# Decay sums without padding, gathered by two DMAs, in an RWKV-6 attention and maxout kernel

## The chip, the cores and the metric

The kernel runs on one core of a Trainium2 chip. A core has TensorE (PE, with its weight loads shown apart as PEld), VectorE (DVE), ScalarE (ACT), GpSimd (POOL) and SyncE (SP), each with its own instruction queue, and 16 DMA engines that move data between the core's memories and HBM. The metric is device time in microseconds (us) of one execution.

## The reference

The first part is a linear attention with a decay for each channel, the second a feed-forward layer without a bias:

```python
# r, k, v, w: (B=4, H=8, S=768, D=48); u: (H, D)
for t in range(S):
    cur = einsum('bhd,bhe->bhde', u[None] * kt, vt)
    y[:, :, t] = einsum('bhd,bhde->bhe', rt, state + cur)
    state = wt[:, :, :, None] * state + einsum('bhd,bhe->bhde', kt, vt)
x = y.transpose(0, 2, 1, 3).reshape(B * S, H * D)        # 3072 x 384
out = maximum(x @ w1, x @ w2) @ w_out                    # d_ff = 1024
```

## The kernel before

The time axis is cut into three segments of 256 steps (`SEG`). Two neighbouring steps sit in one partition, so that a segment fills 128 partitions. A unit is one segment of one or two batches (`UNITS`): units 0 to 3 are the first segment of one batch each, units 4 and 5 the second segment of two batches each, units 6 and 7 the last segment. In each unit the recurrence is turned into matrix products: scores of r against k under a mask, products with v, and a state per head (`S_f`, 48 x 48 values) that passes from one segment to the next.

The decay runs through the logarithm. `wp` multiplies the decays of the two steps of a pair, `ln` takes the logarithm into `lg`, `ex` sums `lg` over the earlier partitions on PE with the triangle `tri`, `e0` exponentiates this sum in place (`E`), and `mz` (line 323, DVE) adds `lg` to the sum, which gives the sum up to and with the partition's own pair: `MZ`. This has one buffer for all units. `ie` (line 329, ACT) makes exp(-MZ), the factor by which k is scaled.

The last partition of `MZ` holds the sum over the whole segment, one value for each channel. The state needs its exponential as a column: channel on the partition. Six units (all but the two of the last segment) therefore do the following. `row` (line 334, SP) copies partition 127 of `MZ` to DRAM, as one row. `wl` (line 338, SP) reads it back with one element per partition and column: this is the gather. `we` (line 342, ACT) takes the exponential into `W`, and `sm` (line 451, POOL or DVE) multiplies the state by it. The next segment's `st` (line 445) adds to this state.

A head has 48 channels and is kept on 64 partitions (`DP`), two heads to the 128 partitions (`NP` = 4 pairs): head 2p on partitions 0 to 47, head 2p+1 on 64 to 111, and 16 partitions of zeros behind each. Before the change `MZ` itself has 64 columns for each head, of which the last 16 are set to zero once (`zero.m`, lines 185 and 198, DVE), and the row in DRAM is H x 64 = 512 values for each batch. One DMA then spreads them: 128 partitions by 4 columns for a unit of one batch, by 8 for two.

The order of all work is written out by hand in `ORDER`: each entry names an operation, its unit and, behind the @, the engine (a ACT, d DVE, p POOL). An engine does its part of the list in that order. Every plain DMA goes through SP, except two of the last stores: the loads of w, k, r, v (line 297, one for each batch), the weights (237 and 242), the row and the gather, the transposes of `dt` (line 412, from unit 5 on) and the stores of the result (568, 570). The gathers of units 0 and 1 stand among the loads of units 2 and 3, those of 2 and 3 among the loads of units 4 and 5; unit 4's is followed by `row.5`, `os.0.0`, `load.7.w` and `dt.5.0.1`, and ACT does `we.4` just ahead of `xe.4.0`, whose tile `xT` the matmuls `gt.4` (line 530, PE) read. The feed-forward layer is `gt` (line 530), `rl` (540 or 542), `op` (549 and 553) and `oe` (148). The launch code behind line 597 allocates the tensors and is not touched.

Of the kernel before, what the change touches and what calls it, by code (L numbers as in the profile page):

```python
# [8 lines left out]
F32 = mybir.dt.float32  # L9
BF16 = mybir.dt.bfloat16  # L10
AF = mybir.ActivationFunctionType
# [4 lines left out]
@with_exitstack  # L16
def kernel(
    ctx: ExitStack,
    tc: tile.TileContext,
    r: bass.AP,  # L20
    k: bass.AP,
    v: bass.AP,
    w: bass.AP,
    u: bass.AP,
    moe_w1: bass.AP,
    moe_w2: bass.AP,
    moe_w_out: bass.AP,
    out: bass.AP,
):
    nc = tc.nc  # L30
    with tc.manual_schedule(), nc.allow_non_contiguous_dma(reason="one row moved onto partitions"):
        _body(tc, r, k, v, w, u, moe_w1, moe_w2, moe_w_out, out)
# [63 lines left out]
def _body(tc, r, k, v, w, u, moe_w1, moe_w2, moe_w_out, out):  # L96
    nc = tc.nc
    B, H, S, D = r.shape
    P = 128
    Q = P // 2  # L100
    HD = H * D
# [3 lines left out]
    NP = H // 2  # L105
    DP = 64
# [7 lines left out]
    const = tc.alloc_tile_pool(name="cst", bufs=1)  # L114
    wk = tc.alloc_tile_pool(name="wk", bufs=1)
    drp = tc.alloc_tile_pool(name="dr", bufs=2, space=bass.MemoryType.DRAM)
    ps = tc.alloc_tile_pool(name="ps", bufs=1, space=bass.MemoryType.PSUM)

    def wt_(shape, dt, tag, bufs=1):
        return wk.tile(shape, dt, tag=tag, name=tag, bufs=bufs)  # L120
# [14 lines left out]
    vp_ = [const.tile([P, 2, NP, 2, VP], BF16, name=f"vp{i}") for i in range(3)]  # L135
    identq = const.tile([P, Q], BF16)
    M_ = [[const.tile([P, 2, NP, 2, Q], BF16, name=f"M{j}{i}") for i in range(3)] for j in range(2)]
    MZ = const.tile([P, 2, H, DP], F32)
    S_f = const.tile([P, 2, B, NP, D], F32)
    S_b = const.tile([P, 2, B, NP, 2, D], BF16)  # L140
    wd_sb = const.tile([P, KO, d_ff], BF16)
# [34 lines left out]
    def c_zero(*a):  # L176
        x, e = a[0], a[-1]
        n = a[1] if len(a) == 3 else 0

        def zero(t):  # L180
            if e == "a":
                k = t.shape[1]
                nc.scalar.copy(t, zw[:, 0:t.shape[2]].unsqueeze(1).to_broadcast([P, k, t.shape[2]]))
            else:
                (nc.vector if e == "d" else nc.gpsimd).memset(t, 0.0)

        if x == "r":
            zero(rp_[n][:, :, :, :, D:].rearrange("p b i h d -> p (b i h) d"))
        elif x == "k":
            zero(kp_[n][:, :, :, :, D:].rearrange("p b i h d -> p (b i h) d"))  # L190
        elif x == "v":
            t = vp_[n].rearrange("p b q e x -> p (b q e) x")
            zero(t[:, :, D:DP])
            zero(t[:, :, DP + D:])
        elif x == "M":
            zero(M_[n % 2][n // 2].rearrange("p e a i g -> p (e a) (i g)"))
        elif x == "m":
            zero(MZ.rearrange("p b h d -> p (b h) d")[:, :, D:])
        else:
            zero(S_b[:, n].rearrange("p b q e d -> p (b q) (e d)"))  # L200

# [117 lines left out]
        nc.scalar.activation(t, t, AF.Exp)  # L319

    def mz(s, b):
        s.mz = MZ[:, 0:s.nb]
        nc.vector.tensor_add(MZ[:, b, :, 0:D],
                             getattr(s, f"E{b}").rearrange("p (h d) -> p h d", h=H),
                             s.lg[:, b].rearrange("p (h d) -> p h d", h=H))

    def ie(s):
        s.iE = wt_([P, 2, HD], F32, "iE", 2)[:, 0:s.nb]
        nc.scalar.activation(s.iE.rearrange("p b (h d) -> p (b h) d", h=H),  # L329
                             s.mz.rearrange("p b h d -> p (b h) d")[:, :, 0:D], AF.Exp, scale=-1.0)  # L330

    def row(s):
        s.row = drp.tile([1, 2 * H * DP], F32, tag="row", name="row")[:, 0:s.nb * H * DP]
        nc.sync.dma_start(out=s.row, in_=MZ[P - 1:P, 0:s.nb].rearrange("o b h d -> o (b h d)"))

    def wl(s):
        s.WL = wt_([P, 2 * NP], F32, "WL", 2)[:, 0:s.nb * NP]
        nc.sync.dma_start(out=s.WL, in_=s.row.rearrange("o (a x) -> x (o a)", x=P))  # L338

    def we(s):  # L340
        s.W = wt_([P, 2 * NP, 1], F32, "W", 2)[:, 0:s.nb * NP]
# [220 lines left out]
    def os(s, a):  # L562
# [6 lines left out]
        else:  # L569
            (nc.scalar if i else nc.sync).dma_start(out=dst[:, i, :], in_=t[:, i])  # L570

    ops = {"tri": c_tri, "ident": c_ident, "mask": c_mask, "zero": c_zero, "u": u_load,
           "uspread": u_spread, "utake": u_take, "ones": c_ones, "warm": warm,
           "wload": w_load, "woload": wo_load, "wdiff": w_diff, "w2cast": w2_cast,
           "wocast": wo_cast, "w2turn": w2_turn, "w2take": w2_take, "wfold": w_fold,
           "wctake": wc_take}
    unit = {"wp": wp, "ln": ln, "ex": ex, "e0": e0, "mz": mz, "ie": ie, "row": row, "wl": wl,
            "we": we, "rk": rk, "ru": ru, "dg": dg, "di": di, "rw": rw, "kw": kw, "vb": vb,
            "scale": scale, "tr": tr, "te": te, "kv": kv, "st": st, "sm": sm, "sb": sb, "sc": sc,
            "mk": mk, "yi": yi, "ya": ya, "xe": xe, "gt": gt, "rl": rl, "op": op,  # L580
            "oe": oe, "os": os, "load": load, "dt": dt}
    for o in ORDER:
        o, _, e = o.partition("@")
        name, *a = o.split(".")
        a = [int(x) if x.isdigit() else x for x in a] + ([e] if e else [])
# [39 lines left out]
```

## Time and profile before

| | |
|---|---|
| median of 3 runs | 146.85 us |
| the three runs | 147.11, 143.3, 146.85 us |
| the profiled execution, its own time | 146.0 us |
| its span, first to last instruction | 144.3 us |
| mean granted TensorE clock | 1.000 |
| PE, DVE, ACT, POOL busy | 133.0, 110.7, 99.3, 77.1 us |
| DMA | 70790 packets, 31.84 MB, mean 221 GB/s |
| gathers, line 338 | six, landing 4.2 to 7.7 us after issue |

How to read the profile: the busy share of an engine is the time in which it has an instruction under way. The slices cut the span into 40 equal parts, with a digit for the tenths busy in each. Groups show the count, the total busy time and the mean duration of one. A wait names the instruction whose end, by the semaphores, released the waiting one. The chain of work that ended last is followed back from the last instruction, at each step to what released it. SPq is the queue of SP: its instructions issue DMAs, and their length is the time until SP goes on to the next, not the transfer's, which has its own time from issue to landing.

### The profile page before, as it was taken

The page shows a single profiled execution, that of the slowest core. Times are in us where ns is not written, and L with a number is a line of the kernel's source. Part 1 is how long each engine was busy: PE and PEld are TensorE (multiplying, and loading weights), DVE is VectorE, ACT ScalarE, POOL GpSimd, SP SyncE. Part 2 cuts the span into 40 slices and gives each one's busy share as a digit, 9 for nine tenths or more (in the row PEclk, how much of TensorE's full clock was granted, in tenths as well). Part 3 has the DMA queues.
Part 4 walks back from the last instruction along what each step waited for, and adds up shares of the span by engine and source line. Part 5 has one row for each costly group of instructions (what it writes and reads, how often), then busy time and mean ns, then how long its engine had stood idle before and what let it go on. Part 6 is the DMA issues. An engine that isn't in the chain of part 4 may idle for free.

```text
span 144.3 us, 5437 instructions
## 1 busy us (share of the span) xinstructions
PE 133.0 (92%) x2378; PEld 80.6 (56%) x2378; DVE 110.7 (77%) x133; ACT 99.3 (69%) x168; POOL 77.1 (53%) x73
## 2 busy tenths in 40 slices
PE   6995569999999999999999989979999999999991
PEld 2333354577777857765754557435567546654560
DVE  0499989989999989989997999966996599040110
ACT  7869799999799899749946937666582752238211
POOL 8828529880691198459494698909786520000000
PEclk9999999999999999999999999999999999999999
DMA  4999999999999997979999999997909960005032
GB/s 104 312 338 311 351 305 347 320 323 244 321 306 268 268 227 180 263 196 277 244 270 211 177 336 344 209 183 169 337 12 160 215 250 7 0 7 218 8 118 95
DMA packets 70790, 31.84 MB, mean 221 GB/s; under 512 B 67175, under 2 KB 68712, under 8 KB 70766
## 3 DMA queue, kind: packets, MB, share of 16 engines
q1 hardware_dynamic: 70478, 31.10, 83.6%
q8 instruction: 18, 0.29, 0.8%
q10 hardware_dynamic: 288, 0.39, 0.7%
q14 instruction: 6, 0.05, 0.1%
HBM read 23.61 MB, written 4.73 MB: 196 GB/s over the span
## 4 chain that ended last, share of the span: by engine, by line
PE 41%; DVE 20%; DMA 19%; issue 6%; SPq 5%; ACT 4%; POOL 2%; DVEq 0%
PE G L553 13%; PE G L530 11%; DMA lw<-in_w_dram 6%; DVE M L474 6%; PE G L549 5%; DVE rku L152 5%; DMA lk<-in_k_dram 5%; DMA lv<-in_v_dram 4%; DMA lr<-in_r_dram 4%; SPq L338 4%; PE G L224 3%; PE Y L512 3%; PE E L315 2%; PE Y L467 2%; DVE dg L355 2%
## 5 line engine op out<-in xcount | busy, mean ns | idle before, releaser
L553 PE MATMUL G<-wo_sb,gT 128*128 128x384 bf16 x192 | 35.1, 326 | 0.0
L530 PE MATMUL G<-xT,wd_sb 128*128 128x256 bf16 (+1 forms) x192 | 33.8, 326 | 0.3 <-DVE wd_sb L248 0.2
L540 ACT ACTIVATE gT<-G 128x512 bf16<-128x512 f32 x44 | 25.5, 597 | 11.4 <-PE G L530 10.6
L474 DVE CAST_PREDICATED M<-mask,Y 128x1024 bf16<-128x1024 int32 x24 | 28.5, 1216 | 2.4 <-PE Y L467 2.3
L553 PEld LDWEIGHTS <-gT 128*128 128x128 bf16 x192 | 18.8, 98 | 12.4
L530 PEld LDWEIGHTS <-wd_sb 128*128 128x128 bf16 x192 | 18.2, 98 | 12.8 <-DVE wd_sb L248 0.8
L152 POOL TENSOR_TENSOR kp<-lk,iE 128x768 bf16<-128x768 f32 x11 | 20.1, 1845 | 6.0 <-ACT iE L329 5.6
L148 ACT COPY osb<-G 128x384 f32<-128x384 f32 x21 | 9.8, 479 | 12.9 <-PE G L553 12.4
L152 POOL TENSOR_TENSOR lg<-lw 128x768 f32<-128x768 f32 (+1 forms) x6 | 9.5, 1579 | 12.3 <-DMA lw<-in_w_dram 11.3
L152 POOL TENSOR_TENSOR M<-identq,dg 128x512 bf16<-128x512 bf16 x13 | 14.3, 1110 | 3.2 <-DVE dg L355 3.2
L549 PE MATMUL G<-wc_sb,xT 128*128 128x384 bf16 x72 | 15.8, 328 | 0.0
L152 DVE TENSOR_TENSOR rku<-lr,lk 128x768 f32<-128x768 f32 x12 | 13.3, 1125 | 1.5 <-DMA lk<-in_k_dram 0.7
L224 PE MATMUL G<-zw 128*128 128x512 bf16 x40 | 11.6, 428 | 1.4 <-DVE zw L219 1.2
L315 PE MATMUL E<-lg,tri 128*128 128x384 f32 x24 | 10.4, 509 | 2.3 <-issue 1.2
L148 ACT CAST vp<-lv 128x768 bf16<-128x768 f32 x12 | 9.9, 827 | 2.6 <-DMA lv<-in_v_dram 2.4
L152 POOL TENSOR_TENSOR lr<-lr,lw 128x768 f32<-128x768 f32 (+1 forms) x5 | 7.4, 1488 | 7.8 <-DVE rku L152 7.8
L152 DVE TENSOR_TENSOR rp<-lr,E 128x768 bf16<-128x768 f32 x12 | 11.3, 943 | 0.0
L148 ACT COPY qk<-G 128x1024 bf16<-128x1024 bf16 x11 | 11.0, 1008 | 0.4 <-PE G L399 0.4
L355 DVE TENSOR_REDUCE dg<-rku 128x16 f32<-128x768 f32 (+1 forms) x8 | 10.7, 1343 | 0.1
L152 POOL TENSOR_TENSOR rku<-rku,u_b 128x768 f32<-128x768 f32 x5 | 9.1, 1823 | 2.9 <-DVE rku L152 2.9
L467 PE MATMUL Y<-qk 48*64 48x128 bf16 x384 | 8.6, 220 | 1.1 <-DVE M L474 0.7
L148 ACT CAST xT<-Y 128x768 bf16<-128x768 f32 x9 | 7.2, 797 | 3.5 <-PE Y L512 2.8
(79 smaller groups left out, 191.2 us busy)
## 6 DMA issues: line engine op xcount, KB each, us to landing
lw<-in_w_dram SPq DMA_DIRECT2D x12, 384.0 KB, 6.0
lr<-in_r_dram SPq DMA_DIRECT2D x12, 384.0 KB, 5.5
lk<-in_k_dram SPq DMA_DIRECT2D x12, 384.0 KB, 5.0
lv<-in_v_dram SPq DMA_DIRECT2D x12, 384.0 KB, 5.8
out_dram<-osb SPq DMA_DIRECT2D x10, 384.0 KB, 3.5
gT<-in_moe_w_dram SPq DMA_DIRECT2D x4, 512.0 KB, 6.5
lv<-in_moe_w_out_dram SPq DMA_DIRECT2D x4, 384.0 KB, 5.1
wst<-in_moe_w_dram SPq DMA_DIRECT2D x2, 512.0 KB, 6.1
```

Of the source, the lines that this page charges most:

```text
L148: (nc.scalar.copy if e == "a" else nc.vector.tensor_copy if e == "d" else nc.gpsimd.tensor_copy)(o, i)
L152: (nc.vector if e == "d" else nc.gpsimd).tensor_mul(o, a, b)
L224: nc.tensor.matmul(t.rearrange("p (a t) -> p a t", t=P), zw, zw.unsqueeze(1).to_broadcast([P, 4, P]), start=True, stop=True, skip_group_ch ...
L315: nc.tensor.matmul(t[:, 0:HD], tri, s.lg[:, b])
L338: nc.sync.dma_start(out=s.WL, in_=s.row.rearrange("o (a x) -> x (o a)", x=P))
L355: nc.vector.reduce_sum(s.dg.rearrange("p b h o -> p (b h) o"), s.rku.rearrange("p b h i d -> p (b h i) d"), axis=AX.X)
L467: nc.tensor.matmul(t[q * Q:(q + 1) * Q, e, p * P:(p + 1) * P].rearrange("s (i g) -> s i g", i=2), turned(s, 1, b)[d, j, p, q, :], turned(s ...
L474: nc.vector.copy_predicated(t.rearrange("s e p t -> s (e p) t"), mask[:, j].rearrange("s i g -> s (i g)").bitcast(mybir.dt.int32).unsqueez ...
L530: nc.tensor.matmul(t[:, m * n * P:(m + 1) * n * P].rearrange("c (b t) -> c b t", t=2 * P), wd_sb[:, ko, fo * P:(fo + 1) * P], s.xT[:, 0:s. ...
L540: nc.scalar.activation(o, i, AF.Relu)
L549: nc.tensor.matmul(t[:, 0:HD], s.xT[:, b, ko, i * P:(i + 1) * P], wc_sb[:, ko, :], start=(ko == 0), stop=False)
L553: nc.tensor.matmul(t[:, 0:HD], s.gT[:, c:c + P], wo_sb[:, f, :], start=False, stop=(f == FO - 1))
```

## The change

`MZ` loses its padding: 48 columns for each head. The sum of `mz` and the exponential of `ie` then run over tiles without gaps. The row in DRAM has 384 values for each batch. The gather becomes two DMAs, one for the even heads to partitions 0 to 47 and one for the odd heads to 64 to 111. Since the 16 partitions behind each are no longer written by the gather, the target is a tile `WL_` of its own with two slots, which the units take in turn, and `zero.m` sets this tile to zero instead of the padding of `MZ`. `ORDER` stays as it is.

```diff
-    MZ = const.tile([P, 2, H, DP], F32)
+    MZ = const.tile([P, 2, H, D], F32)
+    WL_ = const.tile([P, 2, 2 * NP], F32)
...
         elif x == "m":
-            zero(MZ.rearrange("p b h d -> p (b h) d")[:, :, D:])
+            zero(WL_)
...
     def mz(s, b):
-        s.mz = MZ[:, 0:s.nb]
-        nc.vector.tensor_add(MZ[:, b, :, 0:D],
-                             getattr(s, f"E{b}").rearrange("p (h d) -> p h d", h=H),
-                             s.lg[:, b].rearrange("p (h d) -> p h d", h=H))
+        s.mz = MZ[:, 0:s.nb].rearrange("p b h d -> p b (h d)")
+        nc.vector.tensor_add(s.mz[:, b], getattr(s, f"E{b}"), s.lg[:, b])
 
     def ie(s):
         s.iE = wt_([P, 2, HD], F32, "iE", 2)[:, 0:s.nb]
-        nc.scalar.activation(s.iE.rearrange("p b (h d) -> p (b h) d", h=H),
-                             s.mz.rearrange("p b h d -> p (b h) d")[:, :, 0:D], AF.Exp, scale=-1.0)
+        nc.scalar.activation(s.iE, s.mz, AF.Exp, scale=-1.0)
 
     def row(s):
-        s.row = drp.tile([1, 2 * H * DP], F32, tag="row", name="row")[:, 0:s.nb * H * DP]
+        s.row = drp.tile([1, 2 * HD], F32, tag="row", name="row")[:, 0:s.nb * HD]
         nc.sync.dma_start(out=s.row, in_=MZ[P - 1:P, 0:s.nb].rearrange("o b h d -> o (b h d)"))
 
     def wl(s):
-        s.WL = wt_([P, 2 * NP], F32, "WL", 2)[:, 0:s.nb * NP]
-        nc.sync.dma_start(out=s.WL, in_=s.row.rearrange("o (a x) -> x (o a)", x=P))
+        s.WL = WL_[:, s.n % 2, 0:s.nb * NP]
+        src = s.row.rearrange("o (a e d) -> e d (o a)", e=2, d=D)
+        for e in range(2):
+            nc.sync.dma_start(out=s.WL[e * DP:e * DP + D], in_=src[e])
```

## The prediction

> **What bounds the kernel now.** I read the page's busy shares and slices first, then the stretches of time, then the chain of work that ended last, and last the queue of SP around line 338, the only engine work that the change adds to.
>
> Busy shares and slices:
>
> ```profile
> PE 133.0 (92%) x2378; PEld 80.6 (56%) x2378; DVE 110.7 (77%) x133; ACT 99.3 (69%) x168; POOL 77.1 (53%) x73
> PE   6995569999999999999999989979999999999991
> DMA  4999999999999997979999999997909960005032
> ```
>
> PE is at nine tenths or more from 22 us almost to the end, but for two slices (at 83 and 94 us), and the DMA engines are full up to about 70 us. So there are two stages: loads and PE together up to about 85 us, and PE alone after that.
>
> The stretches of time (PE, PEld, DVE, ACT and POOL busy, then clock, DMA share and GB/s):
>
> ```profile
> 10.00:15.00 5.00, 2.92 (x32) 1.56 (x33) 4.97 (x6) 4.62 (x7) 3.72 (x4) 1.00 1.09 314
> 35.00:40.00 5.00, 5.00 (x69) 3.84 (x68) 4.88 (x8) 4.09 (x9) 2.65 (x2) 1.00 1.15 313
> 70.00:75.00 5.00, 4.89 (x35) 2.76 (x28) 4.96 (x5) 3.29 (x7) 3.66 (x3) 1.00 1.01 241
> 90.00:95.00 5.00, 3.76 (x80) 2.10 (x63) 3.93 (x4) 3.25 (x6) 3.86 (x2) 1.00 1.18 208
> ```
>
> PE has real holes at 10 to 20 us (about 4 us) and at 90 to 95 us (1.24 us). From 25 us to 140 us all its holes sum to 2.7 us. This caps what any relief after 25 us can bring.
>
> The chain, the pieces that touch the changed code:
>
> ```profile
> 7.96 0.27 DVE MZ L185
> 14.71 0.48 DVE MZ L323
> 28.35 4.45 SPq L338
> 53.59 0.64 SPq L338
> 72.41 5.71 DMA lw<-in_w_dram
> ```
>
> Line 338 is the gather that is now split in two. It sits on the chain twice, 5.09 us together, as SP's queue. One of the two pieces is 4.45 us long.
>
> The gather's own view, and where its result is waited for:
>
> ```profile
> L338 SPq DMA_DIRECT2D WL<-row x6: 693/1220/4452, 20.8 to 99.2; - x6
> DMA to landing us min/median/max: 4.2/4.6/7.7
> 71.17 0.79 ACT L148 CAST xT<-Y 128x768 bf16<-128x768 f32 x1
> 73.57 0.21 ACT L342 ACTIVATE W<-WL 128x8 f32<-128x8 f32 x1 [1.62 <-DMA WL<-row]
> 73.69 0.78 ACT L148 CAST xT<-Y 128x768 bf16<-128x768 f32 x1
> 73.60 0.81 PE L315 MATMUL E<-lg,tri 128*128 128x384 f32 x2
> 74.52 1.67 PE L530 MATMUL G<-xT,wd_sb 128*128 128x512 bf16 x7
> ```
>
> Of six gathers, one is waited for: that of unit 4, issued at 68.91 us, landed at 73.55. ACT stands 1.62 us, does the exponential, then casts xT (ends 74.47), and PE starts gt.4.4 on it at 74.52, after the matmul before it ended at 74.41. So at this one place a later landing moves PE, with 0.1 us to spare.
>
> **The change part by part.** The profiled execution took 146.0 us with a span of 144.3; the median of the three runs is 146.85, so the sum below is made on a run 0.6% under the median, and the runs differ among themselves by 2.6% (143.3 to 147.11). A measurement of this kernel tells about 2% from no change, that is, under 143.9 or over 149.8.
>
> *Memset.* 128x256 becomes 128x16 elements: from 272 ns to about the 112 ns of the smallest DVE memset on the page (zw, 128x64), so 0.16 us less on DVE at 8 us. It is a chain piece, and row.1 waits on SP for mz.1 (2.0 us, to 15.21). But the loads behind it go to DMA engines that are full (share 1.09 at 10 to 15 us), so what is late next is the load of lr. Bounds 0 and -0.16; I take 0.
>
> *mz and ie without gaps.* The padded sum takes 551 ns; the same shape without padding, S_f<-Y,S_f at line 445, takes 553. The exponential of 128x768 takes 835 ns, the logarithm of an unpadded 128x768 840. Zero for both.
>
> *The row to DRAM.* 2 or 4 KB become 1.5 or 3 KB. The packet records have one packet per row, 84 ns for one of 2 KB. Under 0.05 us in a landing of some us; zero.
>
> *Fewer gathered elements.* 512 become 384 for the four one-batch units, 1024 become 768 for the two others: 4096 packets of 4 bytes become 3072. The packet records show 9 ns each, over 16 engines 0.58 us less of DMA time in all. In the stages where DMA is full lie five of the six gathers; at most -0.5, at least 0. I take 0, since PE has the holes only before 20 us, where no gather is yet.
>
> *One more issue per unit, six in all.* The floor is the shortest issues of SP: 0.25 us for a row, 0.37 for a load. The ceiling is the gather itself, median 1.22, and 4.45 for the worst. The long issues are not work of SP: the same load takes 0.37 in one place and 2.14 in another, just where the engines are full, so an issue lasts until there is room for its packets. Two halves with a quarter fewer packets need less room, and what is left is the fixed part; nearest are the load and the row: I take 0.4 each. For wl.0 to wl.3 it is covered by transfers already under way (loads land a median 5.6 us after issue) and by their results' slack: W is computed at 28.46, 38.03, 55.08 and 58.56 without a wait for the gather. Without that cover the four would cost 1.6. For wl.5 the landing at 103.43 has 7.5 us to its use at 110.94, and behind it on SP the transposes wait 4.7 us for POOL anyway: 0. For wl.4 there is no cover: the second half lands 0.4 later, ACT's W, then xT, then gt.4.4 shift: +0.4 less the 0.1 to spare, with nothing given back: I keep 0.4. Bounds here -0.5 (a shorter burst) and +1.2. Queued behind it on SP are row.5, the store os.0.0 and the two loads of lw at 71.99; POOL waits 2.1 us for these already and has a hole of 1.5 us behind, so 0.4 is covered there.
>
> *The rotation of SP's semaphores.* In the trace each DMA of SP waits for the landing of the eighth before it. Six more DMAs make this the seventh in old numbering, for eight issues after each gather. Counted so, the smallest margin among the recorded landings is 0.78 us (lr at 27.32). No wait; up to +0.5 if the timing shifts, taken as 0.
>
> *Clearing the two slots.* WL is now written in two slots of one tile; each slot was last read two units before, as with the two buffers. Zero; its failure is rival C.
>
> Sum: 146.0 + 0.4 = 146.4.
>
> A rule speaks against this change. The Trainium skill, page "DMA: Bandwidth & Descriptors", section "Rules for kernel authors", says that two transfers to disjoint partition halves serialize, and to use one transfer over 128 partitions; its anatomy of one DMA gives about 2.0 us of fixed cost (a fit for another issue path). As an estimate from that page the sum would be 146.0 + 2.0 = 148.0. The trace of before has no split gather, so it does not settle this; rival B prices it from rows.
>
> **The rivals.**
>
> B, the halves follow one another in full. The second then lands a full issue (1.08, the gather at 68.91) and a burst later (0.9 to 1.5 us in the packet records) than the one gather did: +2.0 to +2.6 at wl.4, 148.3. For it: landings of 4.6 us for 4 KB show a queue in order. Against: the first half has fewer packets. This is the page's case above.
>
> C, the second half waits for the first to land (both write one tile). At wl.4 that is a whole landing, +4.6 less 0.1, 150.5; if the two chain places at 28 and 53 us pay 4.2 each too, 158.9. Against: the two loads of a two-batch unit write one tile and leave SP back to back (lw at 71.99 and 72.41).
>
> D, slower: SP is itself the bound, and the second issue costs what the first does. Place: the two chain pieces of line 338. Doubled they add 5.09: 151.1; with the median issue, 1.22, at these two and wl.4, 149.7. It decides from 1 us per issue at these three places. For it: SP has hardly a hole up to 100 us, and 4.45 us lie on the chain. Against: the issue lengths follow the DMA load, and PE is 4.6 to 5.0 of 5.0 busy there.
>
> E, faster: with less room needed, the 4.45 us shrinks to the shortest gather issue, 0.69: -3.76, 142.2. Against: PE's holes after 25 us are 2.7 us in all. If the block only shrinks by the quarter of packets, 5.09 x 0.25 = 1.3 less, 144.7, which is case F.
>
> **How the numbers follow.** Forecast 0.47 (its own range 145.0 to 147.6), B 0.14, C 0.07, D 0.18, E 0.06, F 0.08. Faster: E, and 0.04 of F and of the forecast's spread, since one of three runs before was already at 143.3: 0.10. Slower: C, D less the 0.02 that stay under 149.8, and 0.03 of B's upper end: 0.26. Within 2%: the remaining 0.64. The predicted time is the forecast's, 146.4. The range goes from 143.4 (F with 1.3 more from the spread of runs) to 151.2 (D in full); it leaves out E, the upper part of C and some ends, under 0.2.
>
> **What would show it.** Right: twelve issues at the gather's lines, the second of each pair near 0.4 us where DMA is not full, the pair's sum at 28 us no longer than 4.5 to 5; W of unit 4 on ACT waiting 1.6 to 2.4 us, gt.4.4 0.3 to 0.5 later against the matmuls before it; PE's busy time unchanged at 133. Wrong: a wait of SP of 4 us between the halves (C), pairs whose sum is twice the old issue (D), a landing 2 us later (B), a hole of PE that closes before 85 us (E). The whole is wrong if transfers elsewhere shift by more than their slack, above all the loads at 22 to 28 us, where a margin of 0.8 us is all there is.

## The result and the profile after

The changed kernel takes 150.77 us in the median of six runs (149.19 to 151.26), the kernel before 146.53 us of six (143.3 to 148.0). The ratio is 1.045, with an interval of 1.033 to 1.057: slower by more than 2%, and each of the six lies above each of the six before. The ratio is taken over the runs that lie within 1.5% of the fastest of their kernel, and since the kernel before spreads more widely (two of its six are within) it comes out above the ratio of the medians, 1.029; I give both below. The profiled execution of the changed kernel took 150.66 us, with a span of 149.0.

Busy shares, slices and the main DMA queue of the page of the changed kernel:

```profile
PE 135.3 (91%) x2378; PEld 82.2 (55%) x2378; DVE 109.7 (74%) x133; ACT 98.9 (66%) x168; POOL 76.8 (52%) x73
PE   6996568797999779999999999979999999999992
DMA  4999999998999999999989899999946970005022
q1 hardware_dynamic: 69550, 31.10, 87.3%
```

The same queue before the change:

```profile
q1 hardware_dynamic: 70478, 31.10, 83.6%
```

The same 31.10 MB in 928 fewer packets keep the engines busy for longer: 87.3% of 149.0 us is 130.1 us for each of the 16, where 83.6% of 144.3 was 120.6. No term of the prediction adds DMA time. PE's new holes lie between 22 and 56 us.

Where it begins is told by the stretches of time (PE, PEld, DVE, ACT, POOL busy, then clock, DMA share, GB/s). After:

```profile
5.00:10.00 5.00, 5.00 (x18) 2.17 (x17) 3.38 (x8) 3.69 (x7) 2.81 (x9) 1.00 1.20 297
10.00:15.00 5.00, 3.44 (x26) 1.78 (x24) 4.77 (x6) 3.99 (x6) 3.12 (x3) 1.00 1.24 289
50.00:55.00 5.00, 3.00 (x67) 2.38 (x66) 4.96 (x6) 2.60 (x5) 0.06 (x1) 0.92 0.95 242
55.00:60.00 5.00, 5.00 (x43) 3.03 (x42) 2.99 (x5) 3.65 (x8) 4.32 (x3) 0.74 1.08 244
```

Before, for the first of them:

```profile
5.00:10.00 5.00, 5.00 (x20) 1.98 (x19) 3.92 (x8) 3.61 (x7) 2.81 (x9) 1.00 1.08 325
```

From 5 to 15 us the engines are fuller (1.20 and 1.24 against 1.08 and 1.09) and move less (297 and 289 GB/s against 325 and 314). The first gather is issued at 21.75 us. So the loss starts before the first instruction that the change adds (the second half of that gather, at 23.89 us). A share above 1 means that packets of one engine overlap in time.

The gathers themselves, after:

```profile
L338 SPq DMA_DIRECT2D WL__89<-row x12: 435/1030/4237, 21.7 to 105.4; - x12
DMA to landing us min/median/max: 3.5/4.1/4.7
```

and SP around the first two pairs:

```profile
21.75 2.58 SPq L338 DMA_DIRECT2D WL__89<-row  x2
24.44 0.80 SPq L298 DMA_DIRECT2D lw<-in_w_dram  x1
25.28 2.55 SPq L238 DMA_DIRECT2D wst<-in_moe_w_dram  x1
30.97 4.72 SPq L338 DMA_DIRECT2D WL__89<-row  x2
35.79 0.24 SPq L332 DMA_DIRECT2D row<-MZ  x1
```

Twelve issues, the second of each pair 0.43 to 0.92 us, no wait between the halves, and a pair's sum of 4.72 us where the single one took 4.45. The gather lands no later after its issue than before.

What the late loads do is seen in the waits, ACT's and then PE's line of the time order at 52 us (the last bracket is the idle time before, and what ended it):

```profile
52.16 0.83 ACT L149 CAST vp<-lv 128x768 bf16<-128x768 f32 x1 [2.56 <-DMA lv<-in_v_dram]
53.05 0.44 PE L429 MATMUL Y<-vp,kp 64*64 64x48 bf16 x32 [2.00 <-ACT vp L149]
```

v arrives late, ACT casts it late, and PE stands for 2.00 us at a place where before it had no hole. After this the granted clock is 0.74 in the mean of five microseconds. One of the six runs of the changed kernel has a mean clock of 1.000 and takes 150.89 us, so the clock is not what the loss hangs on.

Theory P (placement) was formed from these rows. `MZ` has become 1024 bytes shorter in each partition and `WL_` takes 64, so the tiles allocated behind them start 960 bytes earlier (the last two, `W` and `xT`, behind the old place of `WL`, 1024). In the allocation of the two programs the buffers of the loads (lw, lr, lk, lv) start at multiples of 512 bytes before the change, and 64 bytes past one after it. A load is made of rows of 384 bytes, one packet each. The packet records of the traces show these 49152 packets:

| kernel | load buffers, past a multiple of 512 | mean, ns | at 22 ns | above 22 |
|---|---|---|---|---|
| before | 0 | 22.9 | 97.9% | 1.2% |
| after | 64 | 26.3 | 54.6% | 44.5% |

The packets that are neither at 22 ns nor above it take 20 or 21. 49152 x 3.4 ns over 16 engines are 10.4 us more of each engine's time, about the 9.5 us above. The rival, theory S, is the prediction's case D: the split itself, through SP.

### The profile page after: what moved, and what is told of

It reads as the page before. It is cut to its first block, busy times and chain, and to the rows that moved or that the text cites. A ratio compares the mean times of both kernels' runs of the same rounds, so it can differ in the third digit from the quotient of the medians.

```text
span 149.0 us, 5446 instructions
## 1 busy us (share of the span) xinstructions
PE 135.3 (91%) x2378; PEld 82.2 (55%) x2378; DVE 109.7 (74%) x133; ACT 98.9 (66%) x168; POOL 76.8 (52%) x73
## 3 DMA queue, kind: packets, MB, share of 16 engines
q1 hardware_dynamic: 69550, 31.10, 87.3%
## 4 chain that ended last, share of the span: by engine, by line
PE 66%; DMA 18%; SPq 6%; ACT 4%; DVE 3%; issue 1%
PE G L553 19%; PE G L530 18%; DMA gT<-in_moe_w_dram 9%; DMA lv<-in_v_dram 8%; PE G L549 8%; PE E L316 4%; PE Y L512 4%; PE Y L467 4%; PE G L225 4%; SPq L238 3%; PE Y L500 2%; PE Y L429 2%; SPq L338 2%; PE G L399 1%; ACT qk L149 1%; SPq L298 1%
## 5 line engine op out<-in xcount | busy, mean ns | idle before, releaser
L530 PE MATMUL G<-xT,wd_sb 128*128 128x256 bf16 (+1 forms) x192 | 34.7, 332 | 0.2
L153 DVE TENSOR_TENSOR rku<-lr,lk 128x768 f32<-128x768 f32 x12 | 12.7, 1066 | 4.6 <-DMA lr<-in_r_dram 2.9
L225 PE MATMUL G<-zw 128*128 128x512 bf16 x40 | 12.5, 455 | 1.4 <-DVE zw L220 1.2
L316 PE MATMUL E<-lg,tri 128*128 128x384 f32 x24 | 11.1, 538 | 1.9 <-ACT lg L311 1.1
L324 DVE TENSOR_TENSOR MZ<-E,lg 128x384 f32<-128x384 f32 x12 | 6.6, 553 | 4.5 <-PE E L316 4.4
```

Of the source, the lines that this page charges most:

```text
L153: (nc.vector if e == "d" else nc.gpsimd).tensor_mul(o, a, b)
L225: nc.tensor.matmul(t.rearrange("p (a t) -> p a t", t=P), zw, zw.unsqueeze(1).to_broadcast([P, 4, P]), start=True, stop=True, skip_group_ch ...
L316: nc.tensor.matmul(t[:, 0:HD], tri, s.lg[:, b])
L324: nc.vector.tensor_add(s.mz[:, b], getattr(s, f"E{b}"), s.lg[:, b])
L530: nc.tensor.matmul(t[:, m * n * P:(m + 1) * n * P].rearrange("c (b t) -> c b t", t=2 * P), wd_sb[:, ko, fo * P:(fo + 1) * P], s.xT[:, 0:s. ...
```

## The experiments

Times are medians, with the median of the kernel before on the same chip; ratios are those of the result, with their interval. "Moved" means moved in the memory of the core, by bytes in each partition.

**e1: the change, with the old places.**

```diff
-    WL_ = const.tile([P, 2, 2 * NP], F32)
+    WL_ = const.tile([P, 2, 128], F32)
...
     def wl(s):
+        if "gap" not in Z:
+            Z["gap"] = wt_([P, 16], F32, "gap")
```

> The changed kernel, with the tile WL_ enlarged to 1024 bytes a partition and 64 bytes left free where WL was, so that every other tile starts where it did before the change (in the changed kernel nearly all tiles that lie behind MZ, the load buffers among them, start at 64 bytes past a multiple of 512; before, the load buffers start at a multiple of 512). Theory P, placement: the loss comes from where the buffers lie and not from the second gather. Then this kernel takes 0.99 to 1.01 of the kernel before (about 146.5 us), and the 384-byte packets of the loads have a mean near 22.9 ns, as before the change, not 26.3 as after it. Theory S, split: the six more issues on SP make the loads late by up to 4.7 us; then it takes 1.04 to 1.05 (about 153), whatever the packets do.

Measured: 146.46 us against 147.1; ratio 1.013 (0.998 to 1.027). Mean of the 384-byte packets 23.1 ns, 97.7% at 22. All that the change does is in this kernel, except for the places, and the loss is gone by the medians; by the ratio 1.3% is left, by its interval at most 2.7%.

**e2: the kernel before, moved by 64 bytes.**

```diff
+    gap = const.tile([P, 16], F32)
     S_f = const.tile([P, 2, B, NP, D], F32)
```

> The kernel before, one gather and padded sums, with 64 unused bytes a partition behind MZ, so that all later tiles start 64 bytes later, as far past a multiple of 512 as in the changed kernel. P: 1.04 to 1.05 of the kernel before (about 153 us), the 384-byte packets near 26 ns in the mean and about half of them above 22. S: 1.00, since not one instruction is different.

Measured: 151.07 us against 147.1; ratio 1.043 (1.027 to 1.059). Packets 26.0 ns, 40.2% above 22. Its instructions are those of the kernel before, and it is as slow as the changed one. Its first stretches and its queue:

```profile
5.00:10.00 5.00, 3.89 (x15) 1.49 (x14) 3.51 (x8) 3.79 (x7) 2.82 (x9) 1.00 1.20 297
10.00:15.00 5.00, 3.54 (x27) 1.96 (x25) 4.82 (x6) 3.97 (x6) 3.11 (x3) 1.00 1.24 290
q1 hardware_dynamic: 70478, 31.10, 87.7%
```

Share and rate, 1.20 and 297, then 1.24 and 290, are those of the changed kernel, to the digit in the first row.

**e3: the change, with 64 bytes more in WL_.**

```diff
-    WL_ = const.tile([P, 2, 2 * NP], F32)
+    WL_ = const.tile([P, 2, 16], F32)
```

> The changed kernel with WL_ of 128 instead of 64 bytes a partition: the load buffers start 128 bytes past a multiple of 512. A row of a load is 384 bytes, so rows start by turns at 0 and 128 past a multiple of 256, as before the change, and touch two blocks of 256 bytes each; in the changed kernel they start at 64 and 192 past one and touch two and three by turns. P with blocks of 256 bytes: 0.99 to 1.01, packets near 22.9 ns. P with blocks of 512 bytes or a need for buffers at a multiple of 512: 1.03 to 1.05, packets above 24. S: 1.04 to 1.05.

Measured: 146.5 us against 147.1; ratio 1.013 (1.000 to 1.026). Packets 23.0 ns, 97.7% at 22. So the buffers need no multiple of 512 or 256: 128 past one is as good.

```profile
q1 hardware_dynamic: 69550, 31.10, 82.5%
```

**e4: only the load buffers moved by 64.** Unused tiles of 64 bytes in front of lw and of lv, and of 448 behind lk and behind lv, so that all the rest stays where it was modulo 512.

```diff
...
     def load(s, name):
+        if name == "w" and "gap0" not in Z:
+            Z["gap0"] = wt_([P, 16], F32, "gap0")
+        if name == "v" and "gap2" not in Z:
+            Z["gap2"] = wt_([P, 16], F32, "gap2")
...
     def wp(s, e):
+        if "gap1" not in Z:
+            Z["gap1"] = wt_([P, 112], F32, "gap1")
...
```

(The fourth tile, behind lv, is set in the same way.)

> The kernel before with only the buffers that the loads of w, k, r, v write (lw, lr, lk, lv) moved by 64 bytes, by unused tiles in front of and behind them; all other tiles keep their place modulo 512. P by the loads: 1.03 to 1.05, 384-byte packets near 26 ns. P by another tile (operands of the engines, the stores, the transposes, the weights): 1.00 to 1.01, packets near 22.9. S: 1.00.

Measured: 149.23 us against 147.1; ratio 1.035 (1.025 to 1.045). Packets 26.2 ns, 43.1% above 22; queue 88.1%. The load buffers carry the effect. The packets and the queue's share are those of e2 (26.0 ns, 87.7%), so the other tiles add nothing that the DMA engines show. The intervals of the two times overlap, and whether other tiles add a part of the time in another way is open.

**e5: only the gather split, in two halves of 64 partitions.**

```diff
-        nc.sync.dma_start(out=s.WL, in_=s.row.rearrange("o (a x) -> x (o a)", x=P))
+        src = s.row.rearrange("o (a x) -> x (o a)", x=P)
+        for e in range(0, P, 64):
+            nc.sync.dma_start(out=s.WL[e:e + 64], in_=src[e:e + 64])
```

> The kernel before, with its padded sums and every tile where it was, and only the gather split into two DMAs of 64 partitions each: six more issues on SP and nothing else, not one packet fewer. Theory P (the loss came from where the load buffers lie): 0.99 to 1.01. Rival D of the prediction (SP is the bound, and the second issue costs what the first does): 1.02 to 1.04.

Measured, over 12 runs: 147.21 us against 146.43, by the medians 0.8 us; ratio 1.013 (1.004 to 1.021), which would be 1.9 us. It lies between the two expectations: the split costs something, and not the greater part of the loss.

**e6: eight pieces of 16 partitions.** As e5 with steps of 16.

> The same with the gather in eight DMAs of 16 partitions, 42 more issues on SP instead of six, to make the cost of an issue large enough to read. In the profile of the changed kernel the shorter one of a pair takes 0.44 us on SP in most places, so SP has 18 us more to do. If issues are covered by transfers under way, the time stays within 1.00 to 1.03 of the kernel before; if each is paid in full, 1.10 to 1.14. By the sixth part of the excess, the split of the changed kernel costs 0 to 0.7 us in the first case and 2 to 3 in the second (seven times as many issues added).

Measured: 160.18 us against 146.43; ratio 1.095 (1.088 to 1.101). That is 13.75 us for 42 issues, 0.33 us each, just under the second case.

```profile
L340 SPq DMA_DIRECT2D WL<-row x48: 302/428/3848, 20.9 to 118.9; - x48
q1 hardware_dynamic: 71150, 31.11, 75.0%
```

The median issue is 0.43 us on SP, and the engines' share has fallen to 75%: here SP does hold back the loads. So the cover that the prediction counted on is finite: seven more issues in a row, 3.0 us, use it up. Whether one more is covered stays open. At 0.33 us each, the six issues of the split would cost 2.0 us, which is what e5 gives by its ratio (1.9); by its medians (0.8) more than half is covered. The mean granted clock of these runs is 0.957 to 0.968, against 0.988 in most runs of the kernel before, so the 0.33 us need not all be time on SP.

**e7: the load buffers moved by 32.** As e4, with gaps of 32 and 480 bytes.

> The kernel before with the load buffers moved by 32 bytes instead of the 64 of the earlier run. Rows of 384 bytes then start at 32 and 160 past a multiple of 256 by turns and touch two and three blocks of 256. P with blocks of 256 bytes: as with 64, 1.03 to 1.05, about half of the 384-byte packets above 22 ns. If the start had to be at a multiple of 64 for a write and 64 had been the worst: other than with 64, either all packets slower or none.

Measured: 151.05 us against 146.43; ratio 1.027 (1.018 to 1.036), by the medians 1.032. Packets 26.0 ns, 39.0% above 22. No difference between 32 and 64 can be told. By the medians the load buffers alone cost 4.6 us here, no less than all tiles together in e2 (4.0).

**e8: only lv moved by 64.** As e4 without the first gap and the one at `wp`.

> The kernel before with only lv moved by 64 bytes, the buffers of one of the four loads (and of the weights w_out). P: a quarter of the loads has the longer packets, so the mean of the 384-byte packets is near 23.7 ns, and the time is 1.005 to 1.02 of the kernel before; a jump to 1.035 would say that the buffers of v alone matter, since in the changed kernel's chain the loads of v stand twice for 12 us together.

Measured: 147.13 us against 146.43; ratio 1.005 (1.001 to 1.010). Packets 23.4 ns, 5.7% above 22. That is less than the 23.7 ns expected, and the time is the same within 2%. The effect grows with the loads that are moved; v alone is not the cause.

**e9 and e10: one head's rows whole, its neighbour's in halves.** Load buffers moved by 64, each load in three DMAs, so that the 384-byte packets are those of the even heads alone (e9) or of the odd heads alone (e10).

```diff
...
+            o = t[:, b].rearrange("p (a e) i d -> p e a i d", e=2)
+            x = src[s.b0 + b, :, s.t0:s.t0 + SEG, :].rearrange("(a e) (p i) d -> p e a i d", e=2, i=2)
+            nc.sync.dma_start(out=o[:, 0].rearrange("p a i d -> p a (i d)"),
+                              in_=x[:, 0].rearrange("p a i d -> p a (i d)"))
+            for i in range(2):
+                nc.sync.dma_start(out=o[:, 1, :, i], in_=x[:, 1, :, i])
...
```

> A look at single rows, not at the time: load buffers moved by 64 bytes as in the earlier run, and each load in three DMAs, so that only the rows of the even heads go as packets of 384 bytes and those of the odd heads as two of 192. The rows of even heads start at 64 past a multiple of 256 and touch two blocks of 256 bytes, as rows at 0 and 128 do. P with blocks of 256 bytes: the 384-byte packets are nearly all at 22 ns, although none of them starts at a multiple of 128; if it is the start as such that costs, they are all above 22.

> The same with the odd heads whole: their rows start at 192 past a multiple of 256 and touch three blocks. P with blocks of 256 bytes: the 384-byte packets are nearly all above 22 ns, with a mean near 29 to 31. If it is the start as such that costs: as in the run with the even heads.

Measured: 25.3 ns and 9.3% above 22 for the even heads, 24.0 ns and 2.4% for the odd ones (168.72 and 170.99 us, one run each, with 96 more issues and 24576 more packets; these times say nothing on the rows). The odd heads, which touch three blocks, were to be nearly all slow and are nearly all at 22; it is the even heads, with two, that have more slow packets. With that, the number of blocks of 256 bytes that a row touches falls as the reason. The Trainium skill, page "DMA: Bandwidth & Descriptors", section "How a descriptor splits into AXI transactions", has a descriptor cut at multiples of 256 bytes; by that a row at 192 past a multiple takes three pieces, and these rows, at 24.0 ns in the mean, show no sign of the third. The page speaks of what is read, and here the moved side is the one written.

**e13, e14, e15: the order of the rows.** Each load in two DMAs of whole rows: even heads, then odd heads (e13 moved by 64, e14 at the old places), or heads 0 to 3, then 4 to 7 (e15, moved by 64). Two explanations are set against each other: (i) a packet is slow when it shares a block of 128 bytes with the one before it, (ii) it is slow by where its own row starts.

```diff
...
+            o = t[:, b].rearrange("p (a e) i d -> p e a (i d)", e=2)
+            x = src[s.b0 + b, :, s.t0:s.t0 + SEG, :].rearrange("(a e) (p i) d -> p e a (i d)", e=2, i=2)
+            for e in range(2):
+                nc.sync.dma_start(out=o[:, e], in_=x[:, e])
...
```

> Load buffers moved by 64 bytes, each load in two DMAs: the four even heads, then the four odd ones, all rows as whole packets of 384 bytes. Successive packets of an engine lie 768 bytes apart and share no block. By (i), shared blocks of 128 bytes between successive packets: at least 95% of the packets at 22 ns, mean near 23, and the time that of e14. By (ii), the start of the row: 40 to 45% of the packets above 22, mean near 26, and 1.02 to 1.04 of e14.

> The same two DMAs for a load with the buffers where they were. Both: packets at 22 ns, mean near 23. The time is the base for the other two; 48 more issues on SP, at 0.33 us each by the run with eight pieces up to 16 us, so 1.03 to 1.11 of the kernel before.

> Load buffers moved by 64 bytes, each load in two DMAs: heads 0 to 3, then heads 4 to 7, so that successive packets are neighbours, except at the seam. By (i) and by (ii): 33 to 45% of the packets above 22 ns, mean 25 to 26; by (i) alone it is slower than e13, by 1.02 to 1.04; by (ii) the same as e13.

| | time, us | ratio to before | mean, ns | above 22 |
|---|---|---|---|---|
| e13 | 152.97 | 1.054 (1.041 to 1.067) | 25.1 | 12.7% |
| e14 | 150.54 | 1.035 (1.016 to 1.053) | 23.6 | 1.8% |
| e15 | 150.94 | 1.040 (1.025 to 1.055) | 25.3 | 27.4% |

The kernel before took 146.83 us beside them. Neither explanation comes out whole. With neighbours in succession 27.4% of the packets are slow, with alternate heads 12.7%: the succession matters. But 12.7% are far more than the 5% that (i) allows; the slow packets of e13 are fewer and longer (median 34 ns, against 29 in e15), so that the two means are nearly the same, and e13 is not faster than e15. The time of e13 to e15 does not follow the packets, with 48 more issues on SP in each.

The packet records show one more thing that neither explanation accounts for. The share of slow packets changes along the run. Of those that start between 5 and 15 us 85% are above 22 ns in the changed kernel, 44% in e15, 17% in e13, and 3% in e10; of those between 45 and 55 us it is 24, 29, 11 and 3%. So the start of a row does not make it slow by itself.

**e11 and e12: row and gather off SP.** Built to beat both kernels, after e6 had shown a price for SP's issues. The two DMAs of the kernel before, issued by ACT (e11) or POOL (e12):

```diff
-        nc.sync.dma_start(out=s.row, in_=MZ[P - 1:P, 0:s.nb].rearrange("o b h d -> o (b h d)"))
+        nc.scalar.dma_start(out=s.row, in_=MZ[P - 1:P, 0:s.nb].rearrange("o b h d -> o (b h d)"))
...
-        nc.sync.dma_start(out=s.WL, in_=s.row.rearrange("o (a x) -> x (o a)", x=P))
+        nc.scalar.dma_start(out=s.WL, in_=s.row.rearrange("o (a x) -> x (o a)", x=P))
```

> The kernel before with the row and the gather issued by ACT's queue instead of SP's: twelve issues less on SP. By the run with eight pieces an issue on SP costs 0.33 us of the end (13.7 us for 42), so up to 4 us might be won, 0.97 to 1.0; ACT pays 0.25 to 1.3 us for each instead and holds back its activations where the engines are full, and row waits there for DVE: if that decides, 1.0 to 1.04.

> The kernel before with the row and the gather issued by POOL's queue. SP is relieved as in the run with ACT. POOL, busy 53% of the span, pays instead, and its work behind each (lg, kp, S_f) waits with it. 0.97 to 1.01 if POOL has the room; above 1.02 if the issue there is long, which no run so far shows.

Measured: 145.75 us against 146.46 with ACT, ratio 0.998 (0.992 to 1.005): no difference that can be told. The issue there is short, also where SP's took 4.45 us:

```profile
L338 ACTq DMA_DIRECT2D WL<-row x6: 366/390/469, 20.1 to 99.7; - x6
```

With POOL 153.53 us against 146.46, from 146.21 to 156.03, too wide for a ratio; the issue of a gather takes 0.83 us of POOL itself, and no gain is in sight.

## Why the prediction was wrong, step by step

It said 146.4 us and no change that can be told, with 26 in 100 for slower; it was slower by 2.9 to 4.5%. The time lies in the range, at its upper end.

*The sum has no term for the places.* This is the step that failed. The part on the two slots says that WL is "now written in two slots of one tile" and puts zero; the part on `mz` and `ie` compares durations of engine instructions and puts zero. Neither asks where the tiles behind MZ go when MZ becomes shorter. e1 takes the places back, e3 moves them to 128 past a multiple of 512, and both keep the rest: 146.46 and 146.5 us, against 150.77. e2 keeps the rest of the kernel before and moves the places: 151.07, against 147.1. Placement is shown as the cause of the greater part, 4.0 to 4.3 us by these medians. By the ratios it is 3.2% (4.5 less the 1.3 of e1 and e3) to 4.3% (e2).

*One more issue per unit, +0.4 us.* The term was too small: 0.8 us by the medians of e5, 1.9 by its ratio, inside the bounds of -0.5 and +1.2 in the first case and above them in the second. The second issue of a pair takes 0.44 us in four of six places, as taken, and 0.64 and 0.92 in the others. Where it acts was wrong too. wl.4 was the one place seen without cover; there ACT now waits 0.48 us for the gather instead of 1.62, xT ends at 78.91, and PE starts on it at 80.18, when its own work before is done:

```profile
78.02 0.21 ACT L342 ACTIVATE W<-WL__89 128x8 f32<-128x8 f32 x1 [0.48 <-DMA WL__89<-row]
78.13 0.78 ACT L149 CAST xT<-Y 128x768 bf16<-128x768 f32 x1
79.53 0.81 PE L316 MATMUL E<-lg,tri 128*128 128x384 f32 x2
80.18 2.11 PE L530 MATMUL G<-xT,wd_sb 128*128 128x512 bf16 x9
```

The split shows between 24 and 60 us instead, where the prediction had put it under cover. SP's queue tells how the cover works: starts in us of the same DMA, with what it is later than before in brackets (from unrounded times):

| DMA of SP | before | after | e2, moved alone | e3, the change at 128 |
|---|---|---|---|---|
| load of lw behind the first gather | 21.59 | 24.44 (+2.85) | 23.65 (+2.06) | 23.95 (+2.36) |
| load of lv, unit 2 | 41.18 | 45.66 (+4.48) | 45.46 (+4.28) | 44.43 (+3.25) |
| third gather | 48.69 | 53.31 (+4.62) | 53.50 (+4.81) | 51.35 (+2.66) |
| load of lk, unit 6 | 66.16 | 69.54 (+3.39) | 70.21 (+4.06) | 66.06 (-0.09) |
| last store | 141.46 | 146.20 (+4.74) | 145.75 (+4.29) | 142.06 (+0.60) |

Not all of e3's column is the split's doing: its first gather starts at 22.00 us, 1.21 later than before, ahead of any second half; in e1 and e6, with packets at 22 ns too, it starts at 20.93 and 20.88. e3 is up to 3 us late and has caught up at 66 us. With the slower packets the queue is 3.4 to 5 us late from 41 us on and does not catch up; the engines' share is 87.3 and 87.7% there, against 82.5% in e3. So most of the split's lateness was covered in this one trace, and the cover is a room that another loss can use up; that the two in the changed kernel add less than their sum is seen in the third row. That the cover is whole is not shown: by the ratios e1, e3 and e5 each stay 1.3% slower (by the medians they are 0.4% faster, 0.4% faster and 0.5% slower).

*Memset, mz, ie, row:* zero was right as far as can be seen. mz takes 553 ns now, against 551; the memset takes 72 ns, where the prediction had put about 112. *Fewer packets:* zero, as taken: e3 has 82.5% of the engines where before had 83.6%.

*The rotation of SP's semaphores:* after the change SP waits for the landing of a DMA only at the end of the program, as before; a pair's second half goes out 0.04 to 0.05 us after the first issue ends.

*The rivals.* B (a landing 2 us later) is out: 4.1 us in the median after issue, against 4.6 before, and at unit 4 ACT goes on with the gathered values 4.78 us after the first half's issue (73.24), against 4.66 before. C (a wait between the halves) is out, by the same 0.04 to 0.05 us. E (the block at 28 us goes) is out: 4.72 us for the pair. F is out with it. D gave 149.7 to 151.1, and the time is 150.77, but its mechanism, SP, carries only the smaller part: with the gather's issues doubled alone (e5) the time is 147.21. Nor does the chain look as D says. Line 338 was to double from 5.09 us on it; after the change it has 2.54 us there, at another place, and two loads of v have 12.14 us:

```profile
21.75 2.10 SPq L338
23.89 0.44 SPq L338
37.42 5.66 DMA lv<-in_v_dram
45.66 6.48 DMA lv<-in_v_dram
```

Had there been no experiment, the number would have spoken for the wrong cause.

*The signs.* Two that were to show the forecast right came out although it was wrong: the second issue near 0.4 us, and 4.72 us for the pair at 28 us. The one named last for the whole being wrong came out too, transfers elsewhere that shift by more than their slack: the load of lw behind the first gather starts 2.85 us later, and the loads of v after it hold up ACT and PE.

*PE's holes as a cap.* The 2.7 us of holes after 25 us bounded what a gain could be. It is no bound for a loss: after the change PE stands 2.00 us at one place where it had no hole. The prediction used the cap for a gain alone.

*What stays open:* why a packet costs more. Buffers at 32 and 64 bytes past a multiple of 512 have slow packets and those at 0 and 128 do not, the order of the rows has a part in it, and so has something that changes along the run (85% of the packets at 5 to 15 us, 24% at 45 to 55). The two explanations tried are both incomplete.

## What to carry to other kernels

A change in the size of one tile moves every tile allocated behind it, so before pricing an edit of a buffer, write down where the targets of the DMAs start before and after it. When DMA is full and the same bytes take more of the engines' time in the first stretch of the profile, before any instruction that the change adds, look at the places, and undo them alone with an unused tile of some bytes. A number that fits a rival is not its proof: moving the places alone and splitting the gather alone are two small edits, and they told the causes apart.

## What the runs showed of the hardware that I had not expected

A 384-byte packet of a load takes 22 ns in 98 of 100 cases when its buffer starts at 0 or at 128 past a multiple of 512 (before, e1, e3, e5), and when it starts at 32 or 64 past one, 39 to 45 of 100 take longer, most of them 24 to 34 ns (after, e2, e4, e7). In this kernel it costs 2.1 and 4.6 us of 147 with the load buffers alone moved (e4, e7) and 4.0 with all tiles behind MZ (e2), by the medians; with the buffers of one load of four (e8) it is 0.7, the same within 2%.

SP's issue of a gather took 4.45 us at 28 us, and ACT's issue of the same gather 0.37 to 0.47 us in all six places (e11). The engines' share at 25 to 35 us is 1.01 in the first and 1.07 in the second. So the length of an issue there is not that of the DMA that is issued; the two differ in the queue, which on SP has the loads ahead of the gather.
